# Linear attention and an ELU network on one core: the second batch's q turned by transfers, weight slices in another order

## Chip, core and metric

The kernel runs on one core of a Trainium2 chip. The metric is device time in microseconds (us), as the median over runs of the same program. All five engines are used: TensorE (PE) for matrix products, VectorE (DVE), ScalarE (ACT) and GpSimd (POOL) for elementwise work, SyncE (SP) to issue most transfers; ACT and POOL issue some too. Each engine works through its own list of instructions in order and waits on semaphores. Inputs and output are float32 in HBM.

## What is computed

For 8 batches, 8 heads, 576 positions and 64 columns a head: q is softmaxed over its columns, k over its positions, `kv = k_s^T v` for each head, and attention gives `q_s kv`. The result, as 4608 tokens by 512, goes through two layers.

```
q_s = softmax(q, axis=-1);  k_s = softmax(k, axis=2)
kv  = einsum('bhsd,bhse->bhde', k_s, v)
x   = einsum('bhsd,bhde->bhse', q_s, kv)   -> (4608, 512)
h   = x @ w_in                              # 512 -> 2048
g   = where(h > 0, h, exp(min(h, 0)) - 1)
out = g @ w_out                             # 2048 -> 512
```

## The kernel before

Tokens are worked on in blocks of 512: blocks 0 to 7 hold the first 512 positions of batch 0 to 7, and block 8 the 64 left over from each. A block has 16 steps, one for each 128 of the 2048 hidden units. In step s the main loop (`program`, L1146) issues

- `hidden` (L882): four matmuls x by w_in into a PSUM bank (L912), then ACT's exponential (L895, or a Relu and an exponential, L892 and L893, for the steps in `clip`), and on POOL a tensor_scalar (L896);
- `project` of the step three before it (L927): four matmuls by w_out (L933), accumulated over the block;
- `elu` (L917): DVE's combination (L925) that gives the transposed hidden tile GT.

I write h9, p9 for hidden and project of step 9 of block 0. In block 0, p6 is issued right behind h9, p9 behind h12, p10 behind h13.

While block j goes through these steps, the attention of batch j+1 is prepared. Where each piece of that work stands is written out by hand in tables: `START` for batch 0, and for each block a table (`FIRST` for block 0, `SECOND`, `LATER`) which gives for each step three strings of words: what is issued between `hidden` and `project`, between `project` and `elu`, and after `elu`. Since the engines' lists are filled in this order, a word's place sets where its instructions stand in every engine's list and in the queues of the transfers. There is no scheduler; every wait follows from who wrote and who last read each tile.

The words that matter here, for batch 1 in block 0 (A is heads 0 to 3, B heads 4 to 7):

- `load:Q:2:ABR`, `load:K:2:MR`, `load:V:1:RAB`: transfers from HBM on SP's queue (`load`, L267). A batch's q and k go to one of two buffers, v to the only one.
- `w1:a:b`, `w2:a:b`: slices a to b-1 of w_in and w_out, issued from POOL (`load_w1` L252, `load_w2` L259). Slice c of w1 is read first by h c, slice c of w2 by p c. The first slices are loaded in `START`, the rest in block 0.
- `qsub`, `qexp`, `qsum`, `qmul`: the softmax of q; `qmul` (L693) writes the scaled half A or B as float16 into QS.
- `pturn:A` and `pturn:B` (`qturn_first`, L733): eight 128x128 transposes on TensorE from QS into the PSUM bank `AB` (L744); `pwide` (`qwide_first`, L775) copies them on ACT into QT (L788).
- `turn:A` and so on (`qturn`, L719): a transposing transfer on SP's queue from QS to QW (L726; L730 for the left-over rows, QWR); `wide` (`qwide`, L790) copies QW into QT (L855 on ACT, L857 on another engine). Batches 2 to 7 are turned in this way.
- `vconv:A:en` (`vconv_first`, L543): v converted to bfloat16 on engine `en`. `kexp` (L497): k's exponential on ACT.
- `kv:A` (L560): 36 small matmuls into bank `AB`; `kfac` (L608): DVE scales the result into MB; `att:f` (L805): MB by QT into bank `AB`; `xc:f` (L814): ACT copies it to XT, the input of the next block's `hidden`.

`kv`, `att`, the turns on TensorE and `rest0` (L864) all use the one bank `AB`, so each of them also waits until the one before has been copied out.

Of the kernel before, what the change touches and what calls it, by code (L numbers as in the profile page):

```python
# [11 lines left out]
B, H, S, D = 8, 8, 576, 64  # L12
# [3 lines left out]
R = 4  # L16
# [19 lines left out]

AT = {"rawA": 0, "rawA2": 1, "rawB": 7, "rawB2": 4, "rawS": 3, "rawT": 2,
      "kturnA": 4, "kturnB": 5, "kvA": 6, "kvB": 4, "pturnA": 5, "pturnB": 5,  # L40
      "att0": 6, "att1": 2, "att2": 3, "att3": 4, "clip": (1, 2, 4, 6, 8, 10, 11, 17, 21, 30, 32, 33, 37, 42, 44)}
START = ("load:Q:0:1 load:K:0:0 load:K:0:1 warm:1:7 warm:4:7 qmax:1 warm:2:4 load:Q:0:3 qsub:1:dve "
# [26 lines left out]
SECOND = {
# [51 lines left out]
class Gen:  # L121
# [760 lines left out]
    def hidden(self, j, c):  # L882
# [34 lines left out]
    def elu(self, j, c):  # L917
# [290 lines left out]
```

## Time and profile before

| | |
|---|---|
| three runs | 309.59, 309.68, 310.59 us; median 309.68 |
| profiled execution | span of 308.1 us from its first to its last instruction; no other time of it is given, and about 1.6 us separate it from the median |
| PE busy | 97% of the span, 1733 matmuls |
| DVE, ACT, POOL busy | 76%, 63%, 56% |
| PEclk | 9 (90% or more of full speed) in all 40 slices |
| moved by DMA | 51.63 MB; HBM read 38.27 MB, written 9.45 MB |

How to read the rows below. A timeline row has the start and the length in us from the span's start, the engine (SPq is SyncE issuing transfers), the line of the kernel, the operation, what it writes and reads, how many, and in brackets how long the engine sat idle before it and what ended that. The matmuls overlap, so four that follow one another take about 0.91 us though their row says 1.07 or more. A row of a transfer has what it writes and reads, the queue, how many, KB each, and the median time in us from its issue to its landing. In the row of the chain the shares are of the span.

### The profile page before, as it was taken

Reading aid. Unit: us, or ns where it says so; the run is one execution under the profiler, and the core shown is the slowest. Engines: PE = TensorE matmul, PEld = TensorE weight load, DVE = VectorE, ACT = ScalarE, POOL = GpSimd, SP = SyncE. Lnnn points to the kernel's source line nnn. Section 1 sums busy time; section 2 is a strip of 40 time slices with the busy share of each in tenths; the row PEclk is TensorE's granted clock in tenths of the full one; section 3 lists DMA queues with packets and bytes.
Section 4 is the critical chain, followed back from the end, with each engine's and each line's share of the span. In section 5 each row is a group of like instructions: output and inputs, shape, how many; then the busy total and the mean of one; then the engine's idle time right before and its main releaser. Section 6 shows DMA issues by size and latency. Waiting matters only on the chain.

```text
span 308.1 us, 4839 instructions
## 1 busy us (share of the span) xinstructions
PE 297.6 (97%) x1733; PEld 240.1 (78%) x1733; DVE 235.0 (76%) x400; ACT 192.9 (63%) x358; POOL 171.3 (56%) x215
## 2 busy tenths in 40 slices
PE   7789899999999999999999999999999999999995
PEld 4467677788878888888888888888888888888884
DVE  6988978979959897999889988998895353335442
ACT  2678975577559784877587758775877543334432
POOL 2968873686436743786278637863686333333440
PEclk9999999999999999999999999999999999999999
DMA  7999999985708993768475846590512030003004
GB/s 261 393 340 364 372 345 257 273 253 145 191 3 246 261 251 105 223 122 231 133 217 144 208 143 209 146 198 3 172 23 57 2 136 0 0 2 136 0 0 136
DMA packets 60584, 51.63 MB, mean 168 GB/s; under 512 B 26897, under 2 KB 50705, under 8 KB 60561
## 3 DMA queue, kind: packets, MB, share of 16 engines
q1 hardware_dynamic: 52960, 41.23, 47.7%
q0 software_dynamic: 6400, 8.39, 10.5%
q10 hardware_dynamic: 1200, 1.72, 2.0%
q8 instruction: 13, 0.21, 0.3%
q14 instruction: 11, 0.08, 0.1%
HBM read 38.27 MB, written 9.45 MB: 155 GB/s over the span
## 4 chain that ended last, share of the span: by engine, by line
PE 85%; DMA 6%; POOL 4%; ACT 2%; DVE 2%; issue 1%
PE bank L933 40%; PE bank L912 40%; DMA W2S<-in_moe_w_out_dram 5%; PE bank L827 2%; POOL W1S L255 1%; PE bank L598 1%; DMA QR<-in_q_dram 1%; POOL QR L679 1%; POOL QS L708 1%; PE bank L805 1%; DVE KT L326 1%; DVE QF L672 0%; PE bank L560 0%; ACT ES L895 0%; ACT ES L893 0%
## 5 line engine op out<-in xcount | busy, mean ns | idle before, releaser
L933 PE MATMUL bank<-W2S,GT 128*128 128x512 f32 x572 | 153.4, 391 | 1.4 <-DMA W2S<-in_moe_w_out_dram 1.2
L896 POOL TENSOR_SCALAR ES<-ES 128x512 f32<-128x512 f32 (+1 forms) x130 | 85.8, 662 | 117.3 <-ACT ES L895 117.3
L912 PE MATMUL bank<-XT,W1S 128*128 128x512 f32 x512 | 138.4, 392 | 0.5 <-issue 0.3
L925 DVE SCALAR_TENSOR_TENSOR GT<-bank,ES 128x512 fp32r<-128x512 f32 (+1 forms) x130 | 87.9, 681 | 54.4 <-PE bank L912 40.6
L933 PEld LDWEIGHTS bank<-W2S,GT 128*128 128x128 f32 x572 | 106.3, 188 | 23.6 <-DMA W2S<-in_moe_w_out_dram 1.6
L895 ACT ACTIVATE ES<-bank 128x512 f32<-128x512 f32 (+1 forms) x130 | 76.0, 592 | 70.9 <-PE bank L912 70.7
L912 PEld LDWEIGHTS bank<-XT,W1S 128*128 128x128 f32 x512 | 94.1, 188 | 19.9 <-ACT XT L814 0.9
L679 POOL TENSOR_TENSOR QR<-QR,QM 128x512 f32<-128x512 f32 (+1 forms) x21 | 24.9, 1187 | 0.6 <-DVE QM L672 0.5
L684 ACT ACTIVATE QR<-QR 128x1024 f32<-128x1024 f32 (+3 forms) x19 | 19.0, 1006 | 3.1 <-DVE QR L679 3.1
L855 ACT ACTIVATE XT<-bank 128x320 fp32r<-128x320 f32 (+1 forms) x30 | 15.0, 501 | 9.4 <-PE bank L827 9.3
L689 DVE TENSOR_REDUCE QZ<-QR 128x16 f32<-128x1024 f32 (+1 forms) x14 | 18.8, 1343 | 0.6 <-ACT QR L684 0.6
L672 DVE TENSOR_REDUCE QM<-QR 128x16 f32<-128x1024 f32 (+1 forms) x14 | 18.8, 1342 | 0.0
L912 PE MATMUL bank<-XTR,W1S 128*128 128x512 f32 x64 | 16.6, 389 | 0.0
L438 DVE TENSOR_TENSOR KR<-KR,NB 128x512 f32<-128x512 f32 x16 | 14.6, 938 | 0.0
L623 ACT ACTIVATE MB<-bank,KZ 64x64 fp32r<-64x64 f32 x44 | 10.1, 302 | 7.0 <-DVE KZ L614 6.9
L387 DVE TRANSPOSE_TENSOR_REDUCE KM<-KR 128x32 f32<-128x1024 f32 x12 | 14.4, 1226 | 0.0
L857 POOL CAST QT<-QW 128x1024 fp32r<-128x1024 f16 x12 | 12.5, 1039 | 2.9 <-DMA QW<-QS 2.9
L912 PEld LDWEIGHTS bank<-XTR,W1S 128*128 128x128 f32 x64 | 12.0, 188 | 2.5
L892 ACT ACTIVATE ES<-bank 128x512 f32<-128x512 f32 x15 | 8.9, 594 | 7.9 <-PE bank L912 7.9
L827 PE MATMUL bank<-QT,MB 128*128 128x320 f32 (+1 forms) x48 | 12.5, 300 | 0.7 <-ACT XT L855 0.7
L708 POOL TENSOR_TENSOR QS<-QR,QI 128x1024 f16<-128x1024 f32 (+1 forms) x7 | 12.5, 1783 | 0.4 <-DVE QI L691 0.4
L484 ACT ACTIVATE EK<-KR 128x1024 bf16<-128x1024 f32 x12 | 12.6, 1050 | 0.0
(108 smaller groups left out, 262.8 us busy)
## 6 DMA issues: line engine op xcount, KB each, us to landing
out_dram<-OSB SPq DMA_DIRECT2D x30, 256.0 KB, 2.7
KR<-in_k_dram SPq DMA_DIRECT2D x6, 1024.0 KB, 7.7
VR<-in_v_dram SPq DMA_DIRECT2D x6, 1024.0 KB, 6.3
QR<-in_q_dram SPq DMA_DIRECT2D x5, 1024.0 KB, 8.0
KR<-in_k_dram SPq DMA_DIRECT2D x8, 288.0 KB, 6.1
VR<-in_v_dram SPq DMA_DIRECT2D x8, 288.0 KB, 6.6
W1S<-in_moe_w_in_dram POOLq DMA_DIRECT2D x3, 768.0 KB, 9.2
QR<-in_q_dram SPq DMA_DIRECT2D x4, 512.0 KB, 11.2
```

The source lines that it names most:

```text
L672: self.op("dve", lambda: v.tensor_reduce(m, QR, AX.X, ALU.max), self.qkeys(b, part), self.qstat("QM", b, part))
L679: self.op(en, lambda: e.tensor_tensor(QR, QR, m, ALU.subtract), keys + self.qstat("QM", b, part), self.qown(b, part))
L684: self.op("act", lambda: a.activation(QR, QR, AF.Exp), keys, self.qown(b, part))
L689: self.op("dve", lambda: v.tensor_reduce(z, QR, AX.X, ALU.add), self.qkeys(b, part), self.qstat("QZ", b, part))
L708: self.op(en, lambda: e.tensor_tensor(out, QR, z, ALU.mult), keys + self.qstat("QI", b, part), [f"QS{x}" for x in cells])
L827: last = pe.matmul(self.bank[bank][:, a - c0:b - c0], self.MB[f][:, :, :].rearrange("p u d -> p (u d)"), self.QT[:, f, a - f * S:b - f * S ...
L855: self.op("act", lambda: e.activation(out, src, AF.Copy), reads, writes)
L895: self.op("act", lambda: a.activation(ES[:, x], ps[:, x], AF.Exp), [f"bank{bank}"], keys + mark)
L896: self.op("gp", lambda: g.tensor_scalar(ES[:, x], ES[:, x], -1.0, 1.0, ALU.add, ALU.mult), keys, keys)
L912: return pe.matmul(ps, self.W1S[:, kc, c * 128:(c + 1) * 128], x[:, kc, 0:SM], start=(kc == 0), stop=(kc == 3))
L925: self.op("dve", lambda: v.scalar_tensor_tensor(out[:, x], *how), [f"bank{bank}"] + eks + (["FINE"] if n < FINE else []), keys)
L933: return pe.matmul(self.bank[OB[t]][:, :], self.GT[n % NG][:, t * 128:(t + 1) * 128], self.W2S[:, c, :], start=(c == 0), stop=(c == NCH - ...
```

## The change

Only the tables change, no function.

- Batch 1's halves A and B are no longer turned by `pturn` and `pwide`, but by `turn` and `wide`, as in the later batches: `turn:A` in step 9 and `turn:B` in step 10, both ahead of `load:Q:2:ABR` on SP's queue and behind `load:K:2:MR`; `wide:A` on ACT in step 12 (where `pwide:B` stood), `wide:B` on POOL in step 13. The left-over rows (`pturn0:R`, `turn:R`) stay as they were.
- Weights: `w1:13:14`, `w1:9:12`, `w2:6:9`, `w1:12:13`, `w2:9:13`, `w1:14:16`, `w2:15:16`, `w2:13:15` become `w1:9:12`, `w2:6:9`, `w1:12:14`, `w2:9:11`, `w1:14:16`, `w2:11:13` (in step 8), `w2:13:15`, `w2:15:16` (in step 14).
- v of batch 1: `vconv:A` moves from POOL in step 10 to ACT in step 8, `vconv:B` from DVE to POOL, both in step 13.
- In the start, `qmul:3` moves from POOL to DVE and stands ahead of `warm:1:3`.
- The words `kmax2:R`, `ksub:R`, `vconv:R` and `kexp:R`, which issue nothing for batch 1, are dropped.

```diff
 START = (...
-         "qsum:3 vconv:B:gp load:K:1:M qmul:2:gp kexp:B kexp:T kv:A kfac:A:dve pturn:A kv:B "
-         "pwide:A:act kfac:B:act warm:1:3 att:1 att:0 qmul:3:gp pturn:B xc:1:dve xc:0 h:2:4 "
+         "load:V:0:2 qexp:3 w1:6:9 qsum:3 vconv:B:gp load:K:1:M qmul:2:gp kexp:B kexp:T kv:A kfac:A:dve "
+         "pturn:A kv:B pwide:A:act kfac:B:act qmul:3:dve warm:1:3 att:1 att:0 pturn:B xc:1:dve xc:0 h:2:4 "
...
 FIRST = {
-    0: ("qmax:A ksub:R:dve", "", "qsub:0:dve"),
-    1: ("w1:13:14", "w1:9:12", "qsub:1:dve"),
-    2: ("", "qmax0:R", "w2:6:9"),
+    0: ("qmax:A", "", "qsub:0:dve"),
+    1: ("w1:9:12", "", "qsub:1:dve"),
+    2: ("qmax0:R", "", "w2:6:9"),
     3: ("hold qexp:A", "load:Q:1:B:act", ""),
-    4: ("w1:12:13", "w2:9:13", "load:K:1:R qsum:A qsub0:R:dve"),
-    5: ("w1:14:16", "kturn", "kacross vconv:R qmax:C"),
+    4: ("w1:12:14", "w2:9:11", "qsum:A qsub0:R:dve"),
+    5: ("w1:14:16", "kturn", "kacross qmax:C"),
     6: ("", "qmul:A hold", "load:V:1:RAB"),
     7: ("qexp0:R", "", "diag qsub:2:dve"),
-    8: ("qsub:D", "kspread load:K:2:MR copy ksub:1 qsum0:R", "qexp:C qmulr0:dve ksub:0 qsum:C"),
-    9: ("pturn:A", "", "ksub:3 kexp:R qmul:B:dve pwide:A:act"),
-    10: ("", "pturn0:R pwide0:R:act", "ksub:2:dve vconv:A:gp"),
+    8: ("qsub:D", "kspread load:K:2:MR copy ksub:1 w2:11:13 qsum0:R", "qexp:C vconv:A:act qmulr0:dve ksub:0 qsum:C"),
+    9: ("turn:A", "", "ksub:3 qmul:B:dve"),
+    10: ("turn:B", "pturn0:R pwide0:R:act", "ksub:2:dve"),
     11: ("rest0 rcopy0:act", "kexp:A", ""),
-    12: ("pturn:B w2:15:16", "pwide:B:act load:Q:2:ABR", "w2:13:15"),
-    13: ("kv:A vconv:B:dve", "kfac:A:dve", "kexp:B peak2:B att:0 xc:0"),
-    14: ("kv:B kfac:B:dve peak2:R qmulr:gp", "att:1 peak2:A", "join2 turn:R xc:1"),
+    12: ("", "wide:A:act load:Q:2:ABR", "w2:13:15"),
+    13: ("vconv:B:gp wide:B:gp kv:A", "kfac:A:dve", "kexp:B peak2:B att:0 xc:0"),
+    14: ("kv:B kfac:B:dve peak2:R qmulr:gp w2:15:16", "att:1 peak2:A", "join2 turn:R xc:1"),
     15: ("att:3", "xc:3", "att:2 load:V:2:MR xc:2 kout2"),
 }
```

More of the change, by code (lines that the diff above doesn't have):

```diff
@@ L33 @@
 VW = 66
[L39 to L42, printed above, removed]
[3 rows of a table removed]
-         "w1:4:6 kacross:B kexp:S vconv:A:act kmin:A qsub:2:gp qsub:3:gp diag:act:B w2:2:3 qsum:0 kmin:B "
-         "kexp:A load:V:0:3 kmin:T qexp:2 qmul:A:dve qsum:2 load:V:0:2 qexp:3 w1:6:9 "
-         "qsum:3 vconv:B:gp load:K:1:M qmul:2:gp kexp:B kexp:T kv:A kfac:A:dve pturn:A kv:B "
-         "pwide:A:act kfac:B:act warm:1:3 att:1 att:0 qmul:3:gp pturn:B xc:1:dve xc:0 h:2:4 "
+AT = {"rawA": 0, "rawA2": 1, "rawB": 7, "rawB2": 4, "rawS": 3, "rawT": 2, "kturnA": 4, "kturnB": 5,
+      "kvA": 6, "kvB": 4, "pturnA": 5, "pturnB": 5, "att0": 6, "att1": 2, "att2": 3, "att3": 4,
+      "clip": (1, 2, 4, 6, 8, 10, 11, 17, 21, 30, 32, 33, 37, 42, 44)}
@@ L50 @@
+START = ("load:Q:0:1 load:K:0:0 load:K:0:1 warm:1:7 warm:4:7 qmax:1 warm:2:4 load:Q:0:3 qsub:1:dve load:Q:0:0 "
+         "kmax:0 warm:3:5 load:K:0:2 kraw:A qexp:1 kmax:1 load:K:0:3 kturn:A load:V:0:1 qmax:0 kraw:S qsum:1 "
+         "qsub:0:gp kacross:A load:Q:0:2 kmax:3 kraw:B kmax:2 load:V:0:0 w1:1:4 w1:0:1 diag:act:A qmax:2 "
+         "kmin:S qexp:0 kraw:T kturn:B w2:0:2 qmax:3 w1:4:6 kacross:B kexp:S vconv:A:act kmin:A qsub:2:gp "
[3 rows of a table added]
          "pwide:B:act w2:3:4 att:2 att:3 xc:2 load:Q:1:A load:Q:1:R w2:4:6 h:0:2 xc:3 kmax2:AB ")
```

4 rows, old and new, of the table START are left out of this document.

## The prediction

> **What bounds the kernel now.** I read the page's chain first, then PE's rows, then each transfer's start and landing.
>
> ```profile
> DMA  7999999985708993768475846590512030003004
> PE bank L933 40%; PE bank L912 40%; DMA W2S<-in_moe_w_out_dram 5%; PE bank L827 2%; POOL W1S L255 1%; PE bank L598 1%; DMA QR<-in_q_dram 1%; POOL QR L679 1%; POOL QS L708 1%; PE bank L805 1%; DVE KT L326 1%; DVE QF L672 0%; PE bank L560 0%; ACT ES L895 0%; ACT ES L893 0%
> ```
>
> The end is a chain of matmuls (L912, L933) with one long transfer in it, of W2. DMA is nine tenths busy until about 54 us (a slice is 7.7 us). Whatever delays PE in block 0 stays in the total; what PE saves there counts only if no later wait of block 0 eats it. PE there:
>
> ```profile
> 35.07 1.09 PE L912 MATMUL bank<-XT,W1S 128*128 128x512 f32 x4
> 36.00 0.62 PE L744 MATMUL bank<-ID,QS 128*128 128x128 f16 x8
> 37.57 1.19 PE L933 MATMUL bank<-W2S,GT 128*128 128x512 f32 x4 [0.95 <-DMA W2S<-in_moe_w_out_dram]
> ...
> 43.16 1.08 PE L912 MATMUL bank<-XT,W1S 128*128 128x512 f32 x4
> 44.09 0.62 PE L744 MATMUL bank<-ID,QS 128*128 128x128 f16 x8
> 44.98 1.20 PE L933 MATMUL bank<-W2S,GT 128*128 128x512 f32 x4 [0.28 <-DMA W2S<-in_moe_w_out_dram]
> ...
> 47.71 1.20 PE L933 MATMUL bank<-W2S,GT 128*128 128x512 f32 x4
> 48.75 0.44 PE L805 MATMUL bank<-QT,MB 128*128 128x512 f32 x1
> ...
> 50.05 0.76 PE L560 MATMUL bank<-VB,EK 64*64 64x66 bf16 x36
> ...
> 55.51 0.73 PE L912 MATMUL bank<-XT,W1S 128*128 128x512 f32 x2 [0.23 <-ACT XT L814]
> ```
>
> The rows are h9, the A turn, p6; h12, the B turn, p9; p10, att:0, kv:B; and the second half of block 1's first hidden tile, where block 0's lateness is handed on.
>
> **The change part by part.**
>
> *Turns off PE, weights in another order (one edit in effect).* Both turns (8 transposes, 0.62 each) stand just ahead of a wait for W2, so taking them away alone gains little; the weights decide.
>
> ```profile
> 25.71 0.76 POOL L262 DMA_DIRECT2D W2S<-in_moe_w_out_dram  x1
> 28.02 0.76 POOL L262 DMA_DIRECT2D W2S<-in_moe_w_out_dram  x1
> ```
> ```profile
> W2S<-in_moe_w_out_dram POOLq DMA_DIRECT2D x1, 1024.0 KB, 16.9
> W2S<-in_moe_w_out_dram POOLq DMA_DIRECT2D x1, 768.0 KB, 11.8
> ...
> W2S<-in_moe_w_out_dram POOLq DMA_DIRECT2D x1, 256.0 KB, 6.5
> ```
>
> So w2:6:9 lands at 25.71+11.8 = 37.5 and w2:9:13 at 28.02+16.9 = 44.9, each where PE starts again. Between the two landings POOL's queue moved 1,280 KB (256 of w1 among them) in 7.4 us, 173 KB/us. After the change 256 KB fewer stand ahead of w2:6:9 and 512 KB fewer must land for chunk 9: 1.5 and 3.0 us earlier by that rate, 36.0 and 41.9. Then p6 starts right behind h9 (35.07+0.91 = 35.98, by the 0.91 from 43.16 to the turn) and gains up to 37.57-35.98 = 1.6; p9 gains a further 44.98-44.07 = 0.9. Most that this edit can give: 2.5 us. If w2:11:13, issued later, were late for p11, that would show behind kv:B; it takes the place of bytes that landed by 44.9 and p11 comes only after kv:B (50.05), so I cost it at nothing. The same for w2:15:16, which moves from step 12 to step 14: the row of 256 KB is this very slice, 6.5 us from issue to landing, and p15 comes four steps of about 1.8 us (two rows of 0.91) behind p11. If either were late, PE would wait for W2 there by the difference.
>
> *Turns on SP's queue.* In the list of SP the two transposing transfers stand behind K's third batch (load:K:2:MR) and ahead of Q's third batch. K is in flight for long:
>
> ```profile
> 33.05 0.44 SPq L293 DMA_DIRECT2D KR<-in_k_dram  x1
> 33.53 5.39 SPq L285 DMA_DIRECT2D KR<-in_k_dram  x2
> 38.96 1.61 SPq L293 DMA_DIRECT2D QR<-in_q_dram  x1
> ```
> ```profile
> KR<-in_k_dram SPq DMA_DIRECT2D x1, 1024.0 KB, 14.3
> KR<-in_k_dram SPq DMA_DIRECT2D x1, 64.0 KB, 14.7
> QR<-in_q_dram SPq DMA_DIRECT2D x1, 512.0 KB, 10.9
> ```
>
> K lands at 33.05+14.3 = 47.4, its rest at 33.53+14.7 = 48.2, and Q, issued at 38.96 where turn:A will now stand, at 49.9. Does a transposing transfer queue behind a load? In a later batch one was issued with K in flight; the second fence has the median of all twelve, most of them with nothing ahead, then that K and that transfer:
>
> ```profile
> 97.89 0.61 SPq L293 DMA_DIRECT2D KR<-in_k_dram  x1
> ...
> 103.86 2.06 SPq L726 DMA_TRANSPOSE QW<-QS  x1
> ```
> ```profile
> QW<-QS SPq DMA_TRANSPOSE x12, 3.2
> ...
> KR<-in_k_dram SPq DMA_DIRECT2D x1, 1024.0 KB, 9.4
> ...
> QW<-QS SPq DMA_TRANSPOSE x1, 4.8
> ```
>
> Mostly it lands 3.2 us after issue; there it landed at 103.86+4.8 = 108.7, 1.4 behind K's 97.89+9.4 = 107.3. That reads as a queue served in order. Bounds for turn:A here: 38.96+3.2 = 42.2 if nothing queues, and about 51 if it also has to share with w2:13:15 (the 10.9 of Q at this place, plus a little). Between them the nearest row is that of the later batch: 1.4 behind K's main part gives 48.8, behind its rest 49.6; I take the middle, 49.2. Turn:B holds the same amount and follows by about its pure time, 3.2 less the 2.06 or so of issue, near 50.5; its source is ready long before:
>
> ```profile
> 40.17 1.77 DVE L708 TENSOR_TENSOR QS<-QR,QI 128x1024 f16<-128x1024 f32 x1
> ```
>
> Q's third batch, now behind both turns, lands later by what they occupy, some 2 to 3 us; its first reader, block 1's qmax, comes behind the hand-over and moves by as much, so nothing is added; without that shift it would be DVE that waits.
>
> The page "VectorE: DVE Perf Modes" of the Trainium skill, section The three transpose paths, gives 1309 ns for one 128x128 transpose on the DMA path; eight in a row would be 10.5 us, an estimate, and turn:A would land at 49.4 even with no queue. The 3.2 us above for eight contradicts it, so it stays out of the sum.
>
> *What waits for turn:A.* ACT is in order, and wide:A stands where pwide:B stood (the second row):
>
> ```profile
> 35.73 1.27 ACT L684 ACTIVATE QR<-QR 128x1280 f32<-128x1280 f32 x1
> ...
> 44.96 1.03 ACT L788 ACTIVATE QT<-bank 128x1024 fp32r<-128x1024 f16 x1
> 47.13 0.60 ACT L895 ACTIVATE ES<-bank 128x512 f32<-128x512 f32 x1 [1.14 <-PE bank L912]
> 47.62 1.16 ACT L497 ACTIVATE EK<-KR 128x1152 bf16<-128x1152 f32 x1
> 49.23 0.60 ACT L814 ACTIVATE XT<-bank 128x512 fp32r<-128x512 f32 x1 [0.45 <-PE bank L805]
> ```
>
> Wide:A (1.03, the same shape) runs from 49.2 to 50.25. Behind it in ACT's list are step 13's exponential, kexp:B and xc:0 (the last three rows). So att:0, which reads what wide:A writes, starts at 50.3 against 48.75. ACT goes on at 50.25 instead of 47.13, with steps of 0.5, 1.1 and 0.6 (from start to start, and the last one's length), and xc:0 frees the bank of att:0 at 52.45; kv:B writes that bank, so it can't start sooner.
>
> *v's conversions.* vconv:B moves from DVE to POOL, behind step 13's tensor_scalar (0.6, which follows the exponential that ends at 50.85, so 51.45), with wide:B behind it.
>
> ```profile
> 15.71 1.16 POOL L857 CAST VB<-VR 128x1152 bf16<-128x1152 f32 x1
> ...
> 40.81 2.14 POOL L857 CAST VB<-VR 128x1152 bf16<-128x1152 f32 x1
> ```
>
> It takes 1.16 to 2.14, so VB is there at 52.6 to 53.6. I take 1.16, because DVE has little to do then (qmul:B, the row of 40.17, ran beside the 2.14). kv:B: 52.6 against 50.05, +2.55. From kv:B to the hand-over PE's and ACT's rows follow one another as before (55.51-50.05 = 5.46), so the hand-over is late by 2.5. wide:B (about 1.03, as wide:A) ends near 53.7 on POOL and is read by att:3, some 3 us behind kv:B: hidden, with over 1 us to spare. DVE loses vconv:B, which frees it while it has nothing urgent: nothing. vconv:A moves from POOL to ACT, in place of pwide:A; it has to wait for V:
>
> ```profile
> 30.87 0.44 SPq L277 DMA_DIRECT2D VR<-in_v_dram  x1
> ```
> ```profile
> VR<-in_v_dram SPq DMA_DIRECT2D x1, 288.0 KB, 7.2
> ```
>
> V's second piece lands at 30.87+7.2 = 38.1, and ACT gets there at 35.73+1.27 = 37.0. Behind it stand three exponential operations of 0.6 and pwide0:R, for which PE's rest0 waits; pwide:A, which it replaces, had no such wait. By these lists rest0 starts near 41.5, while the W2 gain would have let it start 1.3 sooner: up to 1.4 of the 2.5 is given back. Hidden by the wait at att:0; without that cover it counts.
>
> *qmul:3 on DVE in the start.* On POOL the two took 1.03 each in a row:
>
> ```profile
> 16.82 2.06 POOL L708 TENSOR_TENSOR QS<-QR,QF 128x512 f16<-128x512 f32 x2
> ```
>
> DVE does it behind kfac:B's reciprocal, done about when POOL was: between 0.3 sooner (two engines beside each other) and 0.5 later (DVE's queue, with att:1's copy behind it); I take 0, and either is hidden by the same wait.
>
> *Sum.* -2.5 gained before 45 us is swallowed by a transfer that lands by DMA's clock, not PE's; att:0 +1.55, kv:B +2.55, hand-over +2.5. After it PE's list has no slack to take this back. The profiled span is 308.1 and the median 309.68, so 1.6 lie around the span: 308.1+2.5 = 310.6 of span, **312.2 us**.
>
> **The rivals.**
> *1, faster: the turns don't queue.* Turn:A lands at 43.8 (38.96+4.8), ahead of wide:A's turn on ACT. Then the W2 gain shows, less the 1.4 for V: -1.1 at att:0, about -1.2 at the end, 308.5; without V's cost 307.3. For it: 4.8 is the only time under load that was seen; K's bytes may spread so that most are through at 45. Against: the landing counts the last piece, and Q at the same place took 10.9. The point that decides is a landing before about 46. Chance 0.22.
>
> *2, no change.* Turn:A lands at 46.7, 2.5 sooner than I take it, and kv:B starts when it did: 309.7. For it: K could come sooner, since fewer bytes of w1 and w2 compete with it ahead of p9. Against: the bytes taken out there come back as w2:11:13 while K is still in flight. Chance 0.12.
>
> *3, slower still: TensorE's clock falls.* PE would stand idle from p10's end (46.6, if most of the gain is used) to 50.3, 3.7 us; the longest idle time in block 0 now is 0.95. The first warm-up row shows the low rate:
>
> ```profile
> 1.67 4.11 PE L1093 MATMUL bank<-GT,ONES 128*128 128x512 f32 x10 [1.67 <-DVE VBR L240]
> ```
>
> That is 0.41 a matmul, against 0.91/4 = 0.23 later. A stretch as long as that row at that rate loses 4.11*(1-0.23/0.41) = 1.8: 314.0. "TensorE: Matmul & The Clock Gate" of the Trainium skill, section Why this matters for your kernels, warns of PE idle gaps over about 3 us; no run here shows one. Chance 0.10.
>
> **How the numbers follow.** The forecast has 0.56, from 311.2 (a landing at 48.2, with the last of K) to 314.0 (51; or 313.2 by 2.14 for vconv:B alone); the rivals 0.22, 0.12 and 0.10. Slower by over 0.3% (0.93 us, about what a measurement of this kernel can tell from no change) is 0.56+0.10 = 0.66, same 0.12, faster 0.22. The range leaves out the better half of rival 1 and the tail of rival 3: 308.0 to 314.6.
>
> **What would show it.** Right: p6 and p9 without idle time behind W2; QW A about 10 us from issue to landing; a new idle time of ACT of 4 us or so, ended by DMA QW<-QS; PE idle before att:0 (3 to 4 us) and before kv:B (about 1); the hand-over 2 to 3 us later; the rest of the span alike. Wrong: QW A landing before 47, or PE waiting at rest0 or p11 instead.

## The result, and the profile after

| | median | lowest to highest | runs |
|---|---|---|---|
| before | 309.63 us | 309.37 to 310.59 | 4 |
| changed | 312.35 us | 311.93 to 314.13 | 4 |

The ratio is 1.0091, with a 95% interval of 1.0069 to 1.0114: slower by 2.7 us. The profiled execution took 311.93 us, with a span of 310.1. Its granted TensorE clock was 1.0; the other three executions had 0.995, 0.994 and 0.989, which matters below.

The timeline of the changed kernel, block 0 (its lines are one lower than before's: L932 is project, L804 att, L559 kv, L725 the transposing transfer):

```profile
36.45 1.09 PE L932 MATMUL bank<-W2S,GT 128*128 128x512 f32 x4
...
38.99 1.17 ACT L854 ACTIVATE VB<-VR 128x1152 bf16<-128x1152 f32 x1 [1.25 <-DMA VR<-in_v_dram]
39.56 7.94 SPq L725 DMA_TRANSPOSE QW<-QS  x2
42.11 0.63 PE L863 MATMUL bank<-QT,MB 128*128 128x64 f32 x4 [1.40 <-ACT QT L854]
...
44.51 1.07 PE L932 MATMUL bank<-W2S,GT 128*128 128x512 f32 x4
...
48.62 1.06 ACT L854 ACTIVATE QT<-QW 128x1024 fp32r<-128x1024 f16 x1 [3.31 <-DMA QW<-QS]
49.82 0.47 PE L804 MATMUL bank<-QT,MB 128*128 128x512 f32 x1 [1.51 <-ACT QT L854]
50.83 1.14 POOL L856 CAST VB<-VR 128x1152 bf16<-128x1152 f32 x1
51.11 0.59 ACT L813 ACTIVATE XT<-bank 128x512 fp32r<-128x512 f32 x1
52.11 0.76 PE L559 MATMUL bank<-VB,EK 64*64 64x66 bf16 x36 [0.91 <-POOL VB L856]
57.57 0.73 PE L911 MATMUL bank<-XT,W1S 128*128 128x512 f32 x2 [0.21 <-ACT XT L813]
```

From its list of transfers (KB each, us from issue to landing), w2:6:9, then K's main part and turn:A:

```profile
W2S<-in_moe_w_out_dram POOLq DMA_DIRECT2D x1, 768.0 KB, 10.0
...
KR<-in_k_dram SPq DMA_DIRECT2D x1, 1024.0 KB, 13.4
...
QW<-QS SPq DMA_TRANSPOSE x1, 9.0
```

p6 (36.45) and p9 (44.51) have no wait for W2 any more; before they started at 37.57 and 44.98. Turn:A, issued at 39.56, lands at 39.56+9.0 = 48.6. ACT sits idle 3.31 for it, att:0 starts at 49.82 instead of 48.75, kv:B at 52.11 instead of 50.05, and the hand-over comes at 57.57 instead of 55.51: 2.06 late. That offset stays to the end of the span (310.1 against 308.1). So the loss arises between p10 and kv:B, and the eight blocks behind it change it by under 0.1.

### The profile page after: what moved, and what is told of

Read it like the earlier page. It is cut to its first block, busy times and chain, and to the rows that moved or that the text cites. A ratio compares the mean times of both kernels' runs of the same rounds, so it can differ in the third digit from the quotient of the medians.

```text
span 310.1 us, 4809 instructions
## 1 busy us (share of the span) xinstructions
PE 297.3 (96%) x1717; PEld 239.6 (77%) x1717; DVE 234.6 (76%) x400; ACT 193.1 (62%) x358; POOL 169.6 (55%) x215
## 3 DMA queue, kind: packets, MB, share of 16 engines
q1 hardware_dynamic: 55072, 41.76, 48.2%
## 4 chain that ended last, share of the span: by engine, by line
PE 85%; DMA 4%; POOL 4%; DVE 2%; issue 2%; ACT 2%; SPq 1%; POOLq 0%; ACTq 0%
PE bank L932 40%; PE bank L911 39%; DMA VR<-in_v_dram 2%; PE bank L826 2%; DMA QR<-in_q_dram 2%; PE bank L597 1%; POOL W1S L254 1%; DVE KT L325 1%; POOL QR L678 1%; POOL VB L856 1%; POOL W2S L261 1%; SPq L276 1%; PE bank L804 0%; PE bank L559 0%; POOL ES L895 0%
## 5 line engine op out<-in xcount | busy, mean ns | idle before, releaser
L932 PE MATMUL bank<-W2S,GT 128*128 128x512 f32 x572 | 153.2, 391 | 0.1
L932 PEld LDWEIGHTS bank<-W2S,GT 128*128 128x128 f32 x572 | 106.4, 188 | 22.2 <-DVE GT L924 0.6
L622 ACT ACTIVATE MB<-bank,KZ 64x64 fp32r<-64x64 f32 x44 | 10.2, 303 | 7.0 <-DVE KZ L613 6.9
L856 POOL CAST QT<-QW 128x1024 fp32r<-128x1024 f16 x13 | 13.6, 1042 | 1.8 <-DMA QW<-QS 1.7
L826 PE MATMUL bank<-QT,MB 128*128 128x320 f32 (+1 forms) x48 | 12.6, 302 | 0.7 <-ACT XT L854 0.7
L483 ACT ACTIVATE EK<-KR 128x1024 bf16<-128x1024 f32 x12 | 12.6, 1051 | 0.0
```

What stands on the lines that cost most here:

```text
L826: last = pe.matmul(self.bank[bank][:, a - c0:b - c0], self.MB[f][:, :, :].rearrange("p u d -> p (u d)"), self.QT[:, f, a - f * S:b - f * S ...
L856: self.op(en, lambda: e.tensor_copy(out, src), reads, writes)
L932: return pe.matmul(self.bank[OB[t]][:, :], self.GT[n % NG][:, t * 128:(t + 1) * 128], self.W2S[:, c, :], start=(c == 0), stop=(c == NCH - ...
```

## The experiments

Each was run beside the kernel before on the same chip; the ratio is against that, with its 95% interval. The kernel before had a median of 309.73 beside the turns, the weight order and v's conversions alone and beside turn:A ahead of K; 309.76 beside v's halves undone, PE kept busy and only half B; 309.93 beside the long idle time filled, the last weights later and the last run here; 310.06 beside the start's edit. Where I compare starts in block 0, note that p0 to p5 of the profiled executions differ by 0 to 1.6 us from before's, with and without the start's edit; what is read is the change from there on. The four parts run alone are the whole change but for the dropped words, to which `load:K:1:R` of step 4 belongs too (SyncE issues the same transfers of K in both kernels), and for `qmax0:R` of step 2, which moves ahead of `project`; neither changes the order of work in any engine's list.

### One part at a time

**The turns alone**, on the kernel before:

```diff
-    9: ("pturn:A", "", "ksub:3 kexp:R qmul:B:dve pwide:A:act"),
+    9: ("turn:A", "", "ksub:3 kexp:R qmul:B:dve"),
-    10: ("", "pturn0:R pwide0:R:act", ...
+    10: ("turn:B", "pturn0:R pwide0:R:act", ...
-    12: ("pturn:B w2:15:16", "pwide:B:act load:Q:2:ABR", "w2:13:15"),
+    12: ("w2:15:16", "wide:A:act load:Q:2:ABR", "w2:13:15"),
-    13: ("kv:A vconv:B:dve", ...
+    13: ("wide:B:gp kv:A vconv:B:dve", ...
```

> The kernel before with only the turns changed: turn:A and turn:B on SP's queue behind K, wide:A on ACT in step 12, wide:B on POOL in step 13; weight slices, v's conversions and the start as before. Theory: QW A lands at 48.5 to 49.3 again, att:0 at 49.8 to 50.3, xc:0 frees its bank near 51.7 and kv:B starts there (v's B half is on DVE and ready): +1.7 at the hand-over, 311.3 (310.9 to 311.8). Rival (the loss comes from the weights or from v's conversions): TensorE loses two sets of transposes and nothing comes in their place, 309.0 to 309.7.

Measured: 313.51 us, ratio 1.0106 (1.0083 to 1.013). The profiled execution took 312.57 at full clock; the other five had 0.989 to 0.999. Its timeline:

```profile
38.15 1.19 PE L933 MATMUL bank<-W2S,GT 128*128 128x512 f32 x4 [1.55 <-DMA W2S<-in_moe_w_out_dram]
...
45.48 1.20 PE L933 MATMUL bank<-W2S,GT 128*128 128x512 f32 x4 [0.66 <-DMA W2S<-in_moe_w_out_dram]
...
49.41 1.06 ACT L855 ACTIVATE QT<-QW 128x1024 fp32r<-128x1024 f16 x1 [3.76 <-DMA QW<-QS]
50.61 0.47 PE L805 MATMUL bank<-QT,MB 128*128 128x512 f32 x1 [1.21 <-ACT QT L855]
52.55 0.76 PE L560 MATMUL bank<-VB,EK 64*64 64x66 bf16 x36 [0.54 <-ACT XT L814]
```

The turns alone lose more than the whole change (3.8 us against 2.7, by the medians). With the old order of the weights, taking 16 transposes off PE only turns them into longer waits for W2 (1.55 and 0.66, against 0.95 and 0.28), and turn:A lands at 49.4, 0.8 later than in the changed kernel. What DMA did meanwhile shows in the busy share of its 16 engines and what they moved, from 46 to 49 us in 40 slices. First the kernel before, then the turns alone:

```profile
DMA  9999999999999999999999999999999999999999
GB/s 225 331 304 277 307 297 335 280 321 321 362 328 324 365 304 341 335 335 324 359 314 300 300 287 273 355 300 382 314 341 410 300 382 300 338 372 294 328 359 355
```
```profile
DMA  9998995599439922222222224120199999999999
GB/s 205 215 195 195 181 171 137 116 126 126 99 82 99 48 48 68 55 51 51 51 51 61 51 48 51 41 24 20 24 195 283 287 283 294 284 250 290 297 280 294
```

While the last of K (landed at 47.6 to 48.5) is worked off ahead of turn:A, the engines move some 50 GB/s from 47.0 to 48.2 and are mostly idle; before they moved some 320 in the same stretch. From 48.2 until turn:A lands, SP's queue moves some 280, all of it in packets under 512 bytes. But the two kernels also differ in what is in flight there:

```profile
39.53 8.72 SPq L726 DMA_TRANSPOSE QW<-QS  x2
48.29 1.13 SPq L293 DMA_DIRECT2D QR<-in_q_dram  x2
```

The issue of the two turns holds SyncE for 8.72, so Q's third batch, in flight from 38.96 on before, is issued only at 48.29. And the weights in flight beside the turn did not come later for it: w2:15:16 and w2:13:15 landed 5.1 and 6.0 after their issue, against 6.5 and 7.4 before. How much of the 50 GB/s is the turn's own doing is not shown by this run. "Advanced Engine Details and Errata" of the Trainium skill, section X-Bar Transpose (TRN2), says that transposing transfers are as fast as regular ones; this trace comes near that from 48.2 on (280 against 320), and the run with turn:A ahead of K, below, does not agree (111).

**The weight order alone**, on the kernel before:

```diff
-    1: ("w1:13:14", "w1:9:12", "qsub:1:dve"),
+    1: ("w1:9:12", "", "qsub:1:dve"),
-    4: ("w1:12:13", "w2:9:13", ...
+    4: ("w1:12:14", "w2:9:11", ...
-    8: (..., "... copy ksub:1 qsum0:R", ...
+    8: (..., "... copy ksub:1 w2:11:13 qsum0:R", ...
-    12: ("pturn:B w2:15:16", ...
+    12: ("pturn:B", ...
-    14: ("... qmulr:gp", ...
+    14: ("... qmulr:gp w2:15:16", ...
```

> The kernel before with only the weight slices in the new order and sizes. Theory: the waits for W2 ahead of p6 (0.95) and p9 (0.28) go; p9 is reached about 1.0 sooner, since the transposes on TensorE stay; time 308.7 (308.4 to 309.2). Rival (the order costs, by w2:11:13 or w2:15:16 landing late): a wait for W2 at p11 or p15, 309.7 or more.

Measured: 309.79 us, ratio 0.9993 (0.998 to 1.0005): no change, where I had expected a gain. Its timeline has two places where the gain goes: turn B on TensorE in block 0, and GpSimd's subtraction of k's maximum for the next batch in block 1.

```profile
43.88 0.62 PE L744 MATMUL bank<-ID,QS 128*128 128x128 f16 x8 [0.79 <-DVE QS L708]
...
66.24 2.42 POOL L438 TENSOR_TENSOR KR<-KR,NB 128x1024 f32<-128x1024 f32 x1 [1.33 <-DMA NB<-kmax_scratch]
```
The second row in the kernel before:
```profile
65.61 2.40 POOL L438 TENSOR_TENSOR KR<-KR,NB 128x1024 f32<-128x1024 f32 x1
```

p6 starts 1.1 sooner, with turn A still ahead of it on PE. Then a new wait of 0.79 for qmul:B takes half of it, and the hand-over is 0.71 sooner (54.80). In block 1 the round trip of k's maximum through memory does not come sooner: its write, issued at 55.17 instead of 55.88, landed at 61.4 in both, with the third batch's loads in flight, and reading it back took 4.8 instead of 3.6. GpSimd now waits 1.33 for it and starts 0.63 later than before. PE's lead falls from 0.74 to 0.39 between 71 and 73 us, soon behind that subtraction, and to 0.12 by the end; that PE loses it to the subtraction is read from the place and not tested.

**v's conversions alone**, on the kernel before:

```diff
-    8: (..., "qexp:C qmulr0:dve ksub:0 qsum:C"),
+    8: (..., "qexp:C vconv:A:act qmulr0:dve ksub:0 qsum:C"),
-    10: ("", "pturn0:R pwide0:R:act", "ksub:2:dve vconv:A:gp"),
+    10: ("", "pturn0:R pwide0:R:act", "ksub:2:dve"),
-    13: ("kv:A vconv:B:dve", ...
+    13: ("vconv:B:gp kv:A", ...
```

> The kernel before with only v's conversions moved: vconv:A to ACT in step 8, vconv:B to POOL in step 13. Theory: ACT waits about 1 us for V, so rest0 is about 0.5 late, and kv:B waits up to 0.5 for POOL's vconv:B; most of it lies beside the waits for W2: 310.0 (309.6 to 310.4). Rival (these moves are the main cost of the change): 311 or more.

Measured: 310.55 us, ratio 1.0014 (1.0001 to 1.0026). In its profile PE is 0.75 behind before's from p0 on, which is not this edit, and 0.73 at the hand-over (56.24): in block 0 the move costs nothing that lasts. Its cost is small and at the edge of what can be told from no change.

**The start's edit alone**, on the kernel before:

```diff
-          "pwide:A:act kfac:B:act warm:1:3 att:1 att:0 qmul:3:gp pturn:B ...
+          "pwide:A:act kfac:B:act qmul:3:dve warm:1:3 att:1 att:0 pturn:B ...
```

> The kernel before with only the start's edit: qmul:3 on VectorE, ahead of warm:1:3, instead of on GpSimd behind att:0. The profiles of the kernels that have this edit begin block 0 0.1 to 1.6 later than the profile of before, those without it 0.0 to 0.8 later, which may be the spread from run to run. Theory (as predicted): no change, 309.7 within 0.3. Rival: VectorE's queue makes it cost up to 0.5 in every run: 310.0 to 310.3.

Measured: 310.18 us, ratio 1.0006 (0.9991 to 1.0021): no change, as predicted.

### Does turn:A wait for K, and would it be early ahead of it?

In the changed kernel the order of landing is the order of issue on SP's queue: K's main part at 47.23, turn:A at 48.59, 1.4 behind it. **Turn:A ahead of K**:

```diff
-    8: ("qsub:D", "kspread load:K:2:MR copy ...
+    8: ("qsub:D", "kspread turn:A load:K:2:MR copy ...
-    9: ("turn:A", "", "ksub:3 qmul:B:dve"),
+    9: ("", "", "ksub:3 qmul:B:dve"),
```

> The changed kernel with one word moved: turn:A stands in step 8 ahead of load:K:2:MR on SP's queue (it stood behind it); turn:B stays behind K. Theory (the turn queues behind K on SP's queue, and wide:A in ACT's list waits for it): QW A lands right behind V's pieces, at 42 to 44 instead of 48.6; ACT's idle time of 3.3 us before wide:A goes; att:0 starts near 48.4 with no wait for QT; kv:B near 49.7 instead of 52.1; time 309.3 (309.0 to 309.9), 2.5 to 3 below the changed kernel. Rival (v's conversions are what costs: ACT waiting for V, vconv:B on POOL ahead of kv:B): att:0's wait goes but kv:B still waits for POOL, time 311 or more. Rival (the transposing transfer itself is slow beside loads, wherever it stands): QW A still lands 8 us or more after its issue beyond V's landing, time about 312.

Measured: 317.0 us (313.55 to 317.79), ratio 1.0225 (1.0204 to 1.0245), the slowest of all; the theory missed by 7.7. The profiled execution is the fastest, 313.55 at a clock of 0.995; the other five took 316.86 or more at 0.988 or 0.989, and no profile shows where they lost the rest. Its list of transfers (turn:A, K's main part, then turn:B), and rows of its timeline:

```profile
QW<-QS SPq DMA_TRANSPOSE x1, 12.6
...
KR<-in_k_dram SPq DMA_DIRECT2D x1, 1024.0 KB, 16.2
...
QW<-QS SPq DMA_TRANSPOSE x1, 10.2
```
```profile
34.44 1.34 SPq L725 DMA_TRANSPOSE QW<-QS  x1
...
43.03 0.66 PE L863 MATMUL bank<-QT,MB 128*128 128x64 f32 x4 [1.73 <-ACT QT L854]
43.50 2.05 PE L932 MATMUL bank<-W2S,GT 128*128 128x512 f32 x4
44.74 5.70 SPq L725 DMA_TRANSPOSE QW<-QS  x1
55.03 1.04 POOL L856 CAST QT<-QW 128x1024 fp32r<-128x1024 f16 x1 [3.57 <-DMA QW<-QS]
```

Turn:A lands at 47.0, only 1.6 sooner than behind K, although it was issued 5 us sooner: V's last piece lands ahead of it at 42.7, and the weights go on beside it. K, behind it, lands at 52.0 instead of 47.3, turn:B behind K at 44.74+10.2 = 54.9, and att:3 waits for that. Two stretches of the same kernel, with the columns busy time (and count) of PE, PE's weight loads, DVE, ACT and POOL, then granted clock, DMA share and GB/s:

```profile
40.09:43.50 3.41, 1.69 (x15) 1.15 (x9) 1.41 (x3) 3.35 (x7) 2.31 (x3) 1.00 1.40 178
43.50:46.91 3.41, 3.41 (x10) 2.73 (x10) 3.08 (x4) 1.95 (x3) 0.14 (x1) 0.50 1.21 111
```

DMA moved 178 and 111 GB/s there; before it moved 347 and 324 in the same two stretches. Here there was work enough: K (35.83 to 52.0) and w2:11:13 (38.31 to 50.3) were in flight all through. So the landings keep the order of issue, but the turn also holds back whatever is behind and beside it, and going first moves the loss to K and to turn:B behind it. The second row shows something else: the granted clock is 0.50, and the four matmuls of p8 (the row at 43.50) take 2.05.

### TensorE's clock

The clock fell behind an idle time of only 1.73 at rest0, well under the 3.7 of the prediction's third rival. **v's first half back on GpSimd**, on the changed kernel, takes away rest0's wait:

```diff
-    8: (..., "qexp:C vconv:A:act qmulr0:dve ksub:0 qsum:C"),
+    8: (..., "qexp:C qmulr0:dve ksub:0 qsum:C"),
-    10: ("turn:B", "pturn0:R pwide0:R:act", "ksub:2:dve"),
+    10: ("turn:B", "pturn0:R pwide0:R:act", "ksub:2:dve vconv:A:gp"),
```

> The changed kernel with one thing undone: v's first half is converted on GpSimd in step 10 again, not on ACT in step 8. Theory: rest0's 1.40 of idle time on PE goes, so p8 to p10 come 1.2 to 1.4 sooner, but att:0 still waits for QW, which lands at about 48.6 whatever PE does; PE's wait there grows from 1.5 to about 2.8 and the hand-over stays at 57.5: the price of the conversion is hidden. On the clock two readings differ. If the idle time at rest0 lets TensorE's clock fall, it is full in every run now and the median is about 311.9 (the time of the changed kernel's execution with the full clock). If it is the idle time ahead of att:0 and kv:B, the clock falls as often or oftener and the median is 312.4 to 313.5. Rival to both: the landing depends on PE's pace and comes sooner too, 311.0 or less.

Measured: 314.47 us (313.83 to 315.98), ratio 1.0155 (1.0131 to 1.0179): two us worse than the changed kernel, which neither reading had. From its timeline, and two stretches:

```profile
44.79 1.21 PE L911 MATMUL bank<-XT,W1S 128*128 128x512 f32 x4 [0.92 <-DVE GT L924]
50.29 1.06 ACT L854 ACTIVATE QT<-QW 128x1024 fp32r<-128x1024 f16 x1 [6.50 <-DMA QW<-QS]
51.49 0.47 PE L804 MATMUL bank<-QT,MB 128*128 128x512 f32 x1 [3.68 <-ACT QT L854]
```
```profile
48.54:51.96 3.42, 0.47 (x2) 0.45 (x3) 0.00 (x0) 1.67 (x3) 0.03 (x1) 1.00 1.22 328
51.96:55.37 3.41, 3.18 (x42) 2.24 (x41) 2.16 (x4) 2.01 (x3) 3.41 (x5) 0.50 0.63 179
```

Turn:A landed at 50.3, 3.0 behind K's 47.2, and att:0 started 1.67 later than in the changed kernel (51.49, 49.82). PE came to that wait only 0.5 sooner (47.81 for 48.31), since it waited 0.92 for DVE ahead of h13. The two together make 3.68 of idle time at one place, and the clock fell behind it (in every execution: 0.989 to 0.995). So most of what this profile loses is the later landing. For that the trace offers a reason: w2:13:15, issued at 44.56 instead of 45.96, moved 0.36 MB from 48.2 to 49.1, while SP's queue moved no packet; in the changed kernel most of these weights moved behind turn:A's landing. No run takes them out of this kernel, so it is not shown.

**PE kept busy**, on the changed kernel, with matmuls whose results are thrown away:

```diff
-    11: ("rest0 rcopy0:act", "kexp:A", ""),
+    11: ("fill:12:4 rest0 rcopy0:act", "kexp:A", ""),
-    13: (..., "kexp:B peak2:B att:0 xc:0"),
+    13: (..., "kexp:B peak2:B fill:14:5 att:0 xc:0"),
-    14: ("kv:B kfac:B:dve ...
+    14: ("fill:15:3 kv:B kfac:B:dve ...
...
+    def fill(self, j, c, times):
+        pe, bank = self.E["pe"], self.hbank(j * NCH + c)
+        def mm():
+            for _ in range(times):
+                last = pe.matmul(self.bank[bank][:, :], self.W1S[:, 0, 0:128], self.XT[0][:, 0, 0:SM],
+                                 start=True, stop=True)
+            return last
...
```

> The changed kernel with matmuls added whose results are thrown away: 4 ahead of rest0, 5 ahead of att:0, 3 ahead of kv:B, 0.23 each, which fill PE's idle time there. Nothing else differs. Theory: the spread of the changed kernel's runs (311.93 to 314.13, granted clock 1.0 to 0.989) comes from TensorE's clock after PE's idle time; with PE kept busy the clock is full in every run, the hand-over stays at 57.5, and the median is about 311.9 with a spread under 1. Rival: the clock falls for another reason, or the spread has nothing to do with it: 312.3, spread 2. If an added group runs over into the work behind it, up to 0.3 is lost.

Measured: 312.49 us (311.92 to 313.83), ratio 1.009 (1.007 to 1.011). Granted clocks of its six executions: 1.0, 1.0, 0.999, 0.999, 0.998 and 0.995. The clock held in five of six, against one of four without the added matmuls, but the time did not fall: the first group itself waited 1.54 for DVE, and in the profile block 0 began 0.27 later than in the changed kernel's. Inconclusive as a time; the clock is another matter. The stretch ahead of rest0 there, the one ahead of kv:B in the changed kernel, and one each from two runs that follow (v's second half on VectorE, and w2 later):

```profile
40.50:43.91 3.41, 1.87 (x11) 1.26 (x10) 2.12 (x2) 2.99 (x7) 1.99 (x2) 1.00 1.19 360
```
```profile
47.60:51.02 3.42, 1.91 (x8) 1.07 (x7) 0.51 (x3) 2.40 (x3) 0.76 (x2) 1.00 1.15 284
```
```profile
47.99:51.40 3.41, 1.40 (x7) 0.87 (x7) 0.86 (x2) 3.14 (x5) 1.30 (x2) 1.00 1.16 329
51.40:54.82 3.42, 3.42 (x41) 2.87 (x42) 3.01 (x7) 0.43 (x1) 2.11 (x4) 0.50 0.86 237
```
```profile
40.93:44.35 3.42, 1.75 (x9) 1.21 (x9) 1.47 (x3) 3.36 (x7) 2.20 (x3) 1.00 1.16 357
44.35:47.76 3.41, 3.41 (x9) 2.67 (x8) 2.78 (x4) 1.83 (x4) 0.00 (x0) 0.50 1.24 190
```

These stretches are cut where the record of the clock allows it: each change of it lies a whole number of 3.413 us behind the start of the full clock. PE's busy time in a stretch decides over the next one: 0.47, 1.40, 1.69 and 1.75 of 3.41 us were followed by half the clock, 1.87 and 1.91 were not. In all fourteen profiles no other stretch between the start of the full clock and the last matmuls has less than 1.87, and none of the others was followed by half the clock. The border is near half. "TensorE: Matmul & The Clock Gate" of the Trainium skill, section Part 1, has the stretch (3413 ns, running on by itself) and the half rate, and the trace agrees; the idle gap of over about 3 us that the page warns of in its section Why this matters for your kernels is more than was needed here (1.73).

The changed kernel, at 1.91, lies just above. Where the stretches fall against its two idle times (1.40 and 1.51) differs from execution to execution, since the first full clock came at 4.7 to 7.7 us in the profiles: that its executions had clocks of 1.0, 0.995, 0.994 and 0.989 is what this would give (one half-rate stretch is 3.41/2/310 = 0.0055), but only one of them was profiled.

To test it, **the long idle time filled**: the run with v's first half on GpSimd, with 12 matmuls ahead of att:0 and none elsewhere.

```diff
-    13: (..., "kexp:B peak2:B att:0 xc:0"),
+    13: (..., "kexp:B peak2:B fill:14:12 att:0 xc:0"),
```

> The run with v's first half on GpSimd again (median 314.47, granted clock 0.989 to 0.995 in every execution, PE idle for 3.68 ahead of att:0), with 12 matmuls of 0.23 added in that idle time, whose results are thrown away. In the ten profiles so far the granted clock fell to half for one stretch of 3.413 behind each stretch of that length in which PE had been busy for 49% or less, and never behind one with 55% or more. Theory: the added matmuls lift the stretch ahead of att:0 from 14% to about 70%, the clock stays above 0.998 in every execution, and the median falls by the cost of one such stretch, 1.4 to 2.0: 312.4 to 313.0, with att:0 where it was. Rival: the clock falls as before, because it is something else than PE's idle time that lowers it: 314.5.

Measured: 313.63 us (312.46 to 314.03), ratio 1.0119 (1.0101 to 1.0137); the granted clock was 0.999 to 1.0 in all five executions, where it had been 0.995 at most without the matmuls. The stretch ahead of kv:B:

```profile
49.03:52.44 3.41, 3.30 (x15) 2.38 (x13) 1.04 (x2) 3.16 (x5) 1.69 (x3) 1.00 1.17 336
```

So PE's idle time is what lowers the clock. The size was wrong: 0.84 of the median came back, not 1.4 to 2.0. The profiled execution, the fastest at 312.46, has turn:A landing at 49.1; the others, with the same clock, took 1.0 to 1.6 longer, and no profile says where.

### Which wait is last ahead of kv:B

**v's second half back on VectorE**, on the changed kernel:

```diff
-    13: ("vconv:B:gp wide:B:gp kv:A", ...
+    13: ("wide:B:gp kv:A vconv:B:dve", ...
```

> The changed kernel with one thing undone: v's second half is converted on VectorE again, as before the change, not on GpSimd. In the changed kernel kv:B started at 52.11, 0.41 after ACT's xc:0 had freed its bank (51.11+0.59 = 51.70), because GpSimd's conversion ended at 51.97. Theory: that conversion is the last thing that kv:B waits for, so kv:B starts at 51.7, the hand-over comes 0.4 sooner (57.1-57.2) and the median falls from 312.35 to about 311.9. Rival: something else (att:3's operand, wide:B) is the next thing that is late and the 0.4 is gone by the hand-over: 312.3.

Measured: 312.83 us (311.73 to 313.61), ratio 1.0092 (1.007 to 1.0114). kv:B waits for its bank alone now:

```profile
51.39 1.20 PE L559 MATMUL bank<-VB,EK 64*64 64x66 bf16 x36 [0.54 <-ACT XT L813]
52.52 2.07 PE L932 MATMUL bank<-W2S,GT 128*128 128x512 f32 x4
```

xc:0 ended at 51.35 and kv:B started at 51.39, so the step is as expected. But the clock was at half from 51.40 (the rows above) and the next project took 2.07. Five of six executions had a granted clock of 0.993 to 0.995; the sixth, 0.998, took 311.73. In this step the 0.4 is there; that the clock takes it from the time rests on that one execution.

**The last weights later**, on the changed kernel:

```diff
-    12: ("", "wide:A:act load:Q:2:ABR", "w2:13:15"),
+    12: ("", "wide:A:act load:Q:2:ABR", ""),
-    14: ("... qmulr:gp w2:15:16", ...
+    14: ("... qmulr:gp w2:13:16", ...
```

> The changed kernel with w2's slices 13 and 14, issued in step 12 there (at 45.96, while turn:A is in flight), moved to step 14 and joined with slice 15. Nothing else differs. Turn:A landed 1.4 behind K's main part in the changed kernel (48.59, K 47.23), and 3.0 behind it in the run with v's first half on GpSimd, where this weight transfer was issued 1.4 sooner (44.56). Theory: what turn:A spends behind K, it shares with these weights; without them it lands at about 47.9 to 48.3, att:0 starts 0.3 to 0.7 sooner, and so does the hand-over (56.9 to 57.3); the median falls by as much, to 311.6 to 312.1, if TensorE's clock does not fall more often. Rival: turn:A is held by K alone and by its own small packets: no change, 312.3; if the weights come late for p13, PE waits for W2 there and it is slower.

Measured: 313.97 us (313.7 to 314.81), ratio 1.0133 (1.0112 to 1.0153). From its list of transfers and its timeline:

```profile
QW<-QS SPq DMA_TRANSPOSE x1, 8.7
```
```profile
59.80 1.19 PE L932 MATMUL bank<-W2S,GT 128*128 128x512 f32 x4 [1.12 <-DMA W2S<-in_moe_w_out_dram]
```

Turn:A took 8.7 instead of 9.0 and landed 1.4 behind K, as in the changed kernel: what it spends behind K there it does not share with these weights, which move behind its landing. This says nothing of the 3.0 of the run with v's first half on GpSimd, where they were issued sooner and moved ahead of it. The weights, issued later, came 1.12 late for p13, which is the price that the slack of this slice hides.

### Only half of the change

**Half A on TensorE, half B by transfer**, with the weights' new order and v converted as before:

```diff
-    9: ("turn:A", "", "ksub:3 qmul:B:dve"),
+    9: ("pturn:A", "", "ksub:3 qmul:B:dve pwide:A:act"),
-    12: ("", "wide:A:act load:Q:2:ABR", ...
+    12: ("", "load:Q:2:ABR", ...
-    13: ("vconv:B:gp wide:B:gp kv:A", ...
+    13: ("kv:A vconv:B:dve", ...
-    14: (..., "att:1 peak2:A", ...
+    14: (..., "att:1 wide:B:gp peak2:A", ...
```

(vconv:A is on GpSimd in step 10.)

> Only half B is turned by transfer; half A is turned on TensorE as before the change, v is converted as before it, and the weights have the changed order. wide:B is on GpSimd in step 14. Theory: all of the loss comes from half A, whose reader (att:0) comes first; QW of half B lands near 49.5, wide:B ends by 51 to 52, and att:3 needs it only at about 53. PE then has the gain of the weight order without the 0.79 wait for qmul:B that the weights alone showed and without eight transposes: hand-over at 53.8 to 54.3 against 55.51, of which the slow transfers of block 1 may take back most, as they did with the weights alone: 308.6 to 309.6. Rival: the loss comes from the transposing transfers as such (all transfers slow down while one is worked off, so K's third batch and Q's come late for block 1), whichever half it is: 310.5 or more.

Measured: 310.72 us (309.96 to 311.18), ratio 1.0024 (1.0008 to 1.0039). About three quarters of the loss are gone, but it isn't the gain I expected. From its timeline:

```profile
49.18 0.50 PE L804 MATMUL bank<-QT,MB 128*128 128x512 f32 x1 [0.92 <-DVE MB L628]
...
53.08 1.05 POOL L856 CAST QT<-QW 128x1024 fp32r<-128x1024 f16 x1
...
54.28 0.47 PE L804 MATMUL bank<-QT,MB 128*128 128x512 f32 x1 [0.64 <-ACT ES L894]
```

Att:0 waits for DVE, which converts v ahead of kfac:A, and att:3 comes late because wide:B stands behind step 14's work on GpSimd and ends at 54.13. (The row names ACT, whose exponential ended at 54.27; 0.15 is also what lay between GpSimd's vconv:B and kv:B in the changed kernel. The next run decides.) Both come from where I had put two words. **The same, with those two words as the changed kernel has them:**

```diff
-    13: ("kv:A vconv:B:dve", ...
+    13: ("vconv:B:gp wide:B:gp kv:A", ...
-    14: (..., "att:1 wide:B:gp peak2:A", ...
+    14: (..., "att:1 peak2:A", ...
```

> Half A on TensorE, half B by transfer, as in the run with only half B, with two words elsewhere: v's second half is converted on GpSimd and wide:B follows it there in step 13, as the changed kernel has them. In the run with only half B att:0 waited 0.92 for DVE (whose conversion of v ran 1.15 there ahead of kfac:A), and att:3 waited 0.64 because wide:B stood behind step 14's tensor_scalar on GpSimd and ended at 54.1, though its source had landed at 49.15. Theory: both waits go, the hand-over comes 1.3 to 1.5 sooner than there, so 1.1 to 1.3 sooner than in the kernel before by the same start, and block 1's transfers (K's third batch, which sets the shift for k's exponential) take back about half, as they did with the weights alone: 308.6 to 309.4, faster than both kernels. Rival: block 1 takes back all of it: 309.7; or POOL waits for QW and delays step 14's hidden tile: 310.5.

Measured: 309.23 us (308.81 to 310.08) against 309.93, ratio 0.9979 (0.9968 to 0.999): faster than both kernels, by 0.7 us over the one before. Its timeline:

```profile
47.81 0.50 PE L804 MATMUL bank<-QT,MB 128*128 128x512 f32 x1
...
49.58 1.04 POOL L856 CAST QT<-QW 128x1024 fp32r<-128x1024 f16 x1 [1.00 <-DMA QW<-QS]
...
54.63 0.73 PE L911 MATMUL bank<-XT,W1S 128*128 128x512 f32 x2 [0.22 <-ACT XT L813]
```

Att:0 has no wait at all and the hand-over is at 54.63, 0.88 sooner than before. Turn:B lands at 49.5, later than turn:A did in the changed kernel; only its reader comes later, so the same transfer costs nothing. GpSimd waits 1.00 for it and has the time. The gain stays to the end, and the granted clock was 0.999 to 1.0 in all executions.

## Why the prediction was right, and where only in its sum

- **Weights:** w2:6:9 landed at 25.40+10.0 = 35.4 (36.0 predicted), and p6 and p9 lost their waits. That this gain would be swallowed by the transfer held. More than that, it is worth nothing alone: the run with the weights alone was 0.71 ahead at the hand-over and 0.12 at the end, with a wait in block 1 that the prediction did not look for.
- **Turn:A behind K:** landed 48.6, predicted 49.2. It landed 1.4 behind K's main part, where I had taken the middle of two readings; the lower (1.4) was right. This is the term of the sum that was mis-sized most, by 0.6, and att:0 (49.82 for 50.3), kv:B (52.11 for 52.6) and the hand-over (+2.06 for +2.5) carry it on.
- **wide:A, xc:0, vconv:B, kv:B:** each as worked out. vconv:B took 1.14 (1.16 taken), and kv:B started 0.14 behind its end, which the sum left out. Undoing it moved kv:B to the end of xc:0, as the two bounds had it.
- **vconv:A on ACT:** rest0 at 42.11 with 1.40 of idle time (41.5 and up to 1.4 predicted). "Hidden by the wait at att:0" is right for this kernel but not the whole of it: taking the wait away made the kernel 2.1 slower, with 1.67 of a later landing in the profile and a clock that fell in every execution.
- **The idle time ahead of att:0:** 1.51, where the signs asked for 3 to 4. The prediction counted it from p10's end at 46.6; with 1.40 spent at rest0 p10 ended near 48.3, and the landing came 0.6 sooner. The wait at rest0, named as a sign of being wrong if it came instead, came besides.
- **qmul:3, w2:11:13, w2:15:16, wide:B:** no cost that shows, as predicted. Turn:B landed at 51.4, not 50.5, and wide:B (51.93) did not wait for it. That Q's third batch lands later added nothing that shows in the offset behind the hand-over.
- **Rival 1 (the turns don't queue):** fell. Even ahead of K turn:A took 12.6, landing at 47.0, so the landing before 46 that it needs didn't come by this order either.
- **Rival 2 (no change):** fell with the landing at 48.6; it needed 46.7.
- **Rival 3 (the clock falls):** its mechanism is real, its point of decision was wrong. I put it at 3.7 us of idle time in a row and gave it 0.10 as a case of its own; it needs PE busy for less than about half of one 3.41 us stretch, and three of the four executions had some of it. The profiled execution, at full clock, took 311.93, so the median lies 0.4 above it. Whether the clock makes that 0.4 is not shown: the execution at 0.994 took 312.05, and with PE kept busy, at 0.998 or more in five of six, the median was 312.49.

The predicted 312.2 and the measured 312.35 agree better than their parts do, and that is partly luck. The span was taken 0.5 too long (310.6, against 310.1 in the profile), nearly all of it the landing. What lies around the span was taken 0.2 too short (1.6, against 311.93-310.1 = 1.8). And the median lies 0.4 above the profiled execution at full clock, which the sum did not look for. The figure to hold against a sum made on one execution at full clock is that of 311.93. One reading of the rows was off without effect: the 0.91 from 43.16 to the turn is 44.09-43.16 = 0.93.

## What to carry to other kernels

Before work is moved from an engine to a transfer, read from the trace what is in flight on that queue and beside it, and how long after the issue the first reader comes: with both halves turned by transfer the hand-over came 2 us late, with half B alone it came 0.9 sooner than before, and half B's reader (att:3) comes some 4 us behind half A's (att:0; 52.10 and 47.81 in the last run). Half A alone was not run. Take the half that has the slack. And where an engine is made faster ahead of a wait that does not move, count its idle time too: behind 3.68 of it the clock fell in every execution, and filling it gave back 0.84 us.

## What was not expected of the hardware

- A transposing transfer of 128x1024 float16 can hold back what is in flight behind and beside it: with turn:A ahead of K DMA moved 178 and then 111 GB/s over two stretches of 3.4 us, where the kernel before moved 347 and 324. Its issue holds SyncE too: the two took 7.94 in the changed kernel, and one took 5.70 with turn:A ahead of K, against 2.06 in a later batch.
- TensorE's clock went to half for one stretch of 3.41 us behind a stretch in which PE was busy for 1.75 us or less, and not behind 1.87 or more. That border comes from six stretches in six kernels, and no stretch of the fourteen profiles goes against it. An idle time of 1.7 us is then enough if it lies within one stretch, and the same kernel can lose or keep its clock by where the stretches fall.
